# Emission by quarter-array products, and r, k, v loaded without padding

## The chip, the cores and the metric

The kernel runs on one core of a Trainium2 chip. The metric is the device time of one execution in microseconds (us). The core has five engines that work side by side: PE (TensorE, matrix products; the loading of weights is listed apart as PEld), DVE (VectorE), ACT (ScalarE), POOL (GpSimd) and SP (SyncE), which here only issues transfers. Each engine runs its own list of instructions strictly in order; between engines, semaphores hold an instruction back until what it reads is there.

## The reference

```python
for t in range(S):                       # B=4, H=8 heads, S=768, D=48
    cur = einsum('bhd,bhe->bhde', u[None] * k[t], v[t])
    y[t] = einsum('bhd,bhde->bhe', r[t], state + cur)
    state = w[None, :, :, None] * state + einsum('bhd,bhe->bhde', k[t], v[t])
x = y as 3072 rows of 384
e_idx = argmax(x @ w_gate)               # 8 experts; gate_w = softmax of the logits at e_idx
x = gate_w * sigmoid(x @ w_output_gate)[e] * (relu(x @ w1[e]) @ w2[e])
out = (silu(x @ m_gate) * (x @ m_val)) @ m_out      # 384 -> 1536 -> 384
```

So there is an attention with a decaying state and a bonus `u`, a mixture of eight experts with one expert for each token, and a gated feed-forward. Everything is float32.

## The kernel before

The first 132 us of the profiled execution are the attention, and what this text is about lies there. The 3072 tokens are 24 tiles of 128, six tiles to each of the four batches, in order. The eight heads stand as four pairs: in every transposed array a pair has one head on partitions 0 to 47 and the other on 64 to 111, and the rows between hold zeros. The host writes that padding into the input `tr` (r and k transposed, 128 partitions by 1024), and pads v to 64 columns a head in `tok`.

For tile i the work is this (names and lines are those of the profile; `yd_all` is one large array from which many buffers are carved, among them all loaded inputs, so they appear under its name):

- SP loads `tr` (L300), r and k by token (L301) and v (L305). There are three buffers for r and k and four for v, so the load of tile i+3 waits until all that reads tile i is done. The list of SP is written by hand and runs in order.
- `ck` = k·u·r (L396, L397), on DVE for tiles 0 to 2 and on POOL after that; its sum by head is `cb` (DVE, L419). POOL also makes `kdT` (L399) and `kdc` (L400), the scaled k; `kdc` needs `wk_tok`, a table made once at the start (L354, copied by ACT out of `pst`). DVE makes `rdT` (L407).
- ACT spreads `cb` over a diagonal, `dsb` (L423, eight instructions a tile), and DVE puts the scores `pss` (PE, L433) over its upper part (copy_predicated, L437).
- PE makes the new state `pskv` (L455; DVE adds it up in `st`, L465), and `psy` = state part (L482) + scores part (L489). ACT copies it as `yT` (L494).
- `emit` gives tile i out: four products of 32 columns, side by side in the array, for the 16 gate logits of each pair (`psl`, L114), four transposes of 128x128 (`psx`, L120), an ACT copy of each (`lT` L116, `xt` L122), the store of `xt` by SP (L123), a transpose back of the logits (`psl2`, listed as psl, L126) and a sum over the four pairs on DVE (`lg`, L127).

These run staggered: in round i come the scores of tile i, the state and output of tile i-1, and the emission of tile i-2. Between them DVE also works off the routing of the batches that are finished (L127 to L260) and the splitting of expert weights (L976). After the last tile's logits, the last routing step releases the experts and then the feed-forward.

At the start, before the first tile, the table of decay powers is made: `wc`, a scan by DVE (L339) and its reciprocals (L343), from these ACT's `wr_ps` (L345) and `we` (L349), then four transposes `pst` and the copy `wk_tok` (L354). [...]

Of the kernel before, what the change touches and what calls it, by code (L numbers as in the profile page):

```python
# [9 lines left out]
F32 = mybir.dt.float32  # L10
# [26 lines left out]
def moe_kernel(ctx, tc, cst, small, tok, tr, u, w1, w2, m_gate, m_val, m_out, out):  # L37
# [71 lines left out]

    def emit(yT, x_rows, lg, pool, ps_m, ps_y):  # L110

        psl = ps_m.tile([P, P], F32, name="psl", tag="m")
        for q in range(NP):
            nc.tensor.matmul(psl[32 * q : 32 * q + 32, :], lhsT=wg[:, q, :], rhs=yT[:, q, :], start=True, stop=True)  # L114
        lT = pool.tile([P, P], F32, name="lT")
        nc.scalar.copy(lT, psl)  # L116

        psx = ps_y.tile([P, H, 64], F32, name="psx", tag="y")
        for q in range(NP):
            nc.tensor.transpose(psx[:, 2 * q : 2 * q + 2, :].rearrange("p h d -> p (h d)"), yT[:, q, :], ident)  # L120
        xt = pool.tile([P, H, D], F32, name="xt")
        nc.scalar.copy(xt, psx[:, :, 0:D])  # L122
        nc.sync.dma_start(out=x_rows, in_=xt.rearrange("p h d -> p (h d)"))  # L123
# [142 lines left out]
    with ExitStack() as actx:  # L266
        actx.enter_context(tc.manual_schedule(engines={mybir.EngineType.SP}))
        acst = actx.enter_context(tc.tile_pool(name="acst", bufs=1))
        apool = actx.enter_context(tc.tile_pool(name="apool", bufs=2))
        ps_m = actx.enter_context(tc.tile_pool(name="ps_m", bufs=2, space=PSUM))  # L270
        ps_c = actx.enter_context(tc.tile_pool(name="ps_c", bufs=1, space=PSUM))
        ps_s = actx.enter_context(tc.tile_pool(name="ps_s", bufs=2, space=PSUM))
        ps_y = actx.enter_context(tc.tile_pool(name="ps_y", bufs=2, space=PSUM))
        ps_r = actx.enter_context(tc.tile_pool(name="ps_r", bufs=1, space=PSUM))
# [37 lines left out]

        u_tok = acst.tile([P, H, D], F32, name="u_tok")
        for i in range(NIO):
# [41 lines left out]

        st_b = [acst.tile([P, NP, 64], F32, name=f"st{i}") for i in range(2)]
        kdc_b = [acst.tile([P, H, 64], F32, name=f"kdc{i}") for i in range(3)]
# [55 lines left out]
        def bonus(i):  # L414
            if i >= NTILE:
                return
            r_t, k_t, rT, kT, rdT, kdT, ck, kdc = S[i]
            cb = apool.tile([P, H], F32, name="cb")
            nc.vector.reduce_sum(cb, ck, axis=AX.X)  # L419

            dsb = apool.tile([P, H, P], F32, name="dsb", bufs=3)
            for h in [*range(0, H, 2), *range(1, H, 2)]:
                nc.scalar.mul(dsb[:, h, :], ident, cb[:, h : h + 1])  # L423
            S[i] = rdT, kdT, kdc, dsb, heads(io_v[i % NV], 64)

        def scores(i):
            rdT, kdT, kdc, dsb, v_t = S[i]

            banks = [(ps_y, "y"), (ps_m, "m")] if i == 1 else [(ps_s, "s")] * 2
            pss = [pool.tile([P, NP, P], F32, name=f"pss{j}", tag=tag) for j, (pool, tag) in enumerate(banks)]  # L430
            for q, j in itertools.product(range(NP), range(2)):
                p0 = 64 * j
                nc.tensor.matmul(  # L433
                    pss[j][:, q, :], lhsT=kdT[p0 : p0 + 64, q, :], rhs=rdT[p0 : p0 + 64, q, :], start=True, stop=True
                )
# [36 lines left out]

        def outputs(i):

            rdT, kdT, kdc, dsb, v_t = S[i]
            c = i % NCH
            psy = ps_y.tile([P, NP, P], F32, name="psy", tag="y")
            if c > 0:
                for q in range(NP):
                    for j in range(2):  # L480
                        pr = slice(64 * j, 64 * j + 64)
                        nc.tensor.matmul(  # L482
                            psy[pr, q, :], lhsT=st_b[i % 2][pr, q, :], rhs=rdT[pr, q, :], start=(q == 0), stop=False,
                            skip_group_check=True,
                        )
            for q in range(NP):
                for j in range(2):
                    p0 = 64 * j
                    nc.tensor.matmul(  # L489
                        psy[p0 : p0 + 64, q, :], lhsT=v_t[:, 2 * q + j, :], rhs=dsb[:, 2 * q + j, :],  # L490
                        start=(c == 0 and q == 0), stop=(q == NP - 1), skip_group_check=True,
                    )
# [29 lines left out]
        def rows_out(i):  # L522
# [6 lines left out]
            lg, mx = lgs[g.start]  # L529
            yield from emit(S.pop(i), x_d[i * P : (i + 1) * P, :], lg[:, i - g.start, :], apool, ps_m, ps_y)  # L530
            if i + 1 == g.stop:
# [22 lines left out]
        with tc.manual_schedule(engines=set(engines)):  # L554
# [55 lines left out]
            for _ in range(KF - 4):  # L610
                next(head)
            moe.transposed(0, more, ps_y, "y")
            for _ in head:
# [83 lines left out]
    def sequential(c):  # L697
# [11 lines left out]
        with tc.For_i(0, B) as b:  # L709
            nc.vector.memset(st, 0.0)  # L710
            with tc.For_i(0, NCH) as ch:
                i = b * NCH + ch
                rk = sq.tile([P, 2, NP, P], F32, name="sq_rk")
                nc.sync.dma_start(
                    out=rk.rearrange("p a q t -> p (a q t)"), in_=tr[bass.ds(i, 1)].rearrange("o p n -> (o p) n")
                )
                yT = sq.tile([P, NP, P], F32, name="sq_y")
                nc.vector.memset(yT, 0.0)
                with tc.For_i(0, P) as t:
                    kv = sq.tile([P, NP, D], F32, name="sq_kv")  # L720
# [620 lines left out]
def _layout(inputs):  # L1341
# [6 lines left out]

    def tokens(a, pad=0):
        a = a.transpose(0, 2, 1, 3)  # L1350
        if pad:
            a = np.concatenate([a, np.zeros(a.shape[:3] + (pad,), a.dtype)], axis=3)
        return a.reshape(b * n, P, -1)

# [8 lines left out]
    def transposed(a):  # L1363
        a = a.reshape(b, h, n, P, d).transpose(0, 2, 1, 4, 3)
        return pair_rows(a, 0).reshape(b * n, P, -1)

# [6 lines left out]
        "small": small,  # L1373
        "tok": np.concatenate([tokens(r), tokens(k), tokens(v, 64 - d)], axis=2),
        "tr": np.concatenate([transposed(r), transposed(k)], axis=2),
        "u": u,
# [28 lines left out]
```

## Time and profile before

| what | us |
|---|---|
| time of the kernel, median of 3 runs | 837.77 (837.74 to 838.23) |
| time of the profiled execution | 840.54 |
| span of the profiled execution | 838.8 |
| PE / DVE / ACT / POOL busy in the span | 812.4 / 509.9 / 352.0 / 210.1 |
| mean granted clock of PE | 0.993 of full speed |

The profile is of one execution, which took 840.54 us, of which 838.8 us are the span from the first to the last instruction on record. Busy time counts neither waits nor the issue of transfers. PE is busy for 97% of the whole span, but that is a mean over stages in which other engines set the pace.

### The profile page before, as it was taken

To read this page: it belongs to the slowest core of one execution; us is meant where nothing else is said; L and a number is where in the kernel's file an instruction comes from. 1 tells how busy PE (TensorE), PEld (TensorE's weight loads), DVE (VectorE), ACT (ScalarE), POOL (GpSimd) and SP (SyncE) were. 2 spreads that over 40 slices of the span, in tenths; PEclk is the share of its full clock that TensorE was granted. 3 is DMA by queue.
4 is the path that set the end of the run, shared out by engine and by line. 5 is a ranking of instruction groups with operands and counts; after the bars stand their busy time and mean duration, and the time that the engine had idled before them with its cause. 6 is when DMAs were issued, how large, how long until landed. Compare 5 with 4: busy or idle time off the path is not lost.

```text
span 838.8 us, 14568 instructions
## 1 busy us (share of the span) xinstructions
PE 812.4 (97%) x5535; PEld 728.6 (87%) x5536; DVE 509.9 (61%) x1097; ACT 352.0 (42%) x794; POOL 210.1 (25%) x206
## 2 busy tenths in 40 slices
PE   7999999998999999999999999999999999999994
PEld 5777779898999999998888888888888888899994
DVE  7679996599998989855554235333433542344531
ACT  4878764565656566544332112212221221122321
POOL 7998951452433422200002000200100020000000
PEclk9999999999999999999999999999999999999998
DMA  8999974566878876432311000100000010000000
GB/s 309 313 335 327 346 240 136 156 195 198 262 238 253 252 239 205 122 102 86 90 52 47 5 1 13 38 1 1 32 20 1 7 38 1 0 19 27 20 1 23
DMA packets 61839, 99.57 MB, mean 119 GB/s; under 512 B 5364, under 2 KB 47872, under 8 KB 61760
## 3 DMA queue, kind: packets, MB, share of 16 engines
q1 hardware_dynamic: 58320, 88.44, 32.5%
q0 software_dynamic: 3440, 10.11, 3.7%
q8 instruction: 45, 0.74, 0.4%
q14 instruction: 34, 0.28, 0.1%
HBM read 82.00 MB, written 16.53 MB: 117 GB/s over the span
## 4 chain that ended last, share of the span: by engine, by line
issue 58%; DVE 15%; PE 11%; DMA 6%; POOL 5%; ACT 2%; SPq 0%; ACTq 0%; POOLq 0%; DVEq 0%
DMA m<-ab 2%; POOL out_dram L1245 2%; DVE w1l L976 2%; PE pss L433 2%; PE psy L489 2%; DVE ab L952 2%; PE psy L482 1%; DVE w2l L976 1%; DVE ab L948 1%; DMA r<-in_w_dram 1%; PE psx L120 1%; DVE ab L943 1%; DVE h L1121 1%; POOL xg L1053 1%; DMA yd_all<-in_tok_dram 1%
## 5 line engine op out<-in xcount | busy, mean ns | idle before, releaser
L1269 DVE TENSOR_TENSOR hv<-pg,hv 128x512 f32<-128x512 f32 (+1 forms) x84 | 51.7, 615 | 155.8 <-ACT hv L1268 155.7
L1245 POOL DMA_INDIRECT out_dram<-ot,tokd x24 | 24.8, 1035 | 452.2 <-DVE ot L1244 448.6
L1268 ACT ACTIVATE hv<-pg 128x512 f32<-128x512 f32 (+1 forms) x84 | 45.1, 537 | 168.3 <-PE pg L1264 168.0
L884 ACT CAST hh<-hv 128x512 fp32r<-128x512 f32 (+1 forms) x84 | 47.0, 559 | 142.1 <-DVE hv L1270 142.1
L1238 PE MATMUL po<-wh,hh 128*128 128x384 f32 x288 | 97.1, 337 | 0.0
L1238 PE MATMUL po<-wh,hl 128*128 128x384 f32 x288 | 97.0, 337 | 0.0
L1238 PE MATMUL po<-wl,hh 128*128 128x384 f32 x288 | 97.0, 337 | 0.0
L1264 PE MATMUL pg<-xh,wh 128*128 128x512 f32 (+1 forms) x252 | 91.1, 362 | 0.0
L1101 PE MATMUL ph<-x,w1h 128*128 128x416 f32 x336 | 91.1, 350 | 0.0
L1264 PE MATMUL pg<-xh,wl 128*128 128x512 f32 (+1 forms) x252 | 90.9, 361 | 0.0
L1264 PE MATMUL pv<-xh,wh 128*128 128x512 f32 (+1 forms) x252 | 90.8, 360 | 0.0
L1264 PE MATMUL pv<-xh,wl 128*128 128x512 f32 (+1 forms) x252 | 90.7, 360 | 0.0
L1264 PE MATMUL pv<-xl,wh 128*128 128x512 f32 (+1 forms) x252 | 90.6, 360 | 0.0
L1264 PE MATMUL pg<-xl,wh 128*128 128x512 f32 (+1 forms) x252 | 90.5, 359 | 0.0
L1101 PE MATMUL py<-h,w2h 128*128 128x416 f32 x336 | 89.7, 352 | 0.0
L885 DVE TENSOR_TENSOR hl<-hv,hh 128x512 fp32r<-128x512 f32 (+1 forms) x84 | 51.7, 616 | 45.4 <-ACT hh L884 45.1
L1270 DVE TENSOR_TENSOR hv<-pv,hv 128x512 f32<-128x512 f32 (+1 forms) x84 | 51.7, 615 | 43.7 <-PE pv L1264 43.1
L949 POOL TENSOR_TENSOR low<-low,exw 128x384 f32<-128x384 f32 x36 | 40.3, 1119 | 106.6 <-DVE exw L945 80.9
L423 ACT ACTIVATE dsb<-cs,cb 128x128 f32<-128x128 f32 x192 | 58.7, 390 | 14.2 <-DVE cb L419 14.2
L1101 PE MATMUL ph<-x,w1l 128*128 128x416 f32 x168 | 60.7, 361 | 3.3 <-DVE h L1121 3.3
L1101 PEld LDWEIGHTS py<-h,w2h 128*128 128x128 f32 x336 | 62.9, 188 | 0.8
L1101 PEld LDWEIGHTS ph<-x,w1h 128*128 128x128 f32 x336 | 63.0, 188 | 0.5
(228 smaller groups left out, 1710.2 us busy)
## 6 DMA issues: line engine op xcount, KB each, us to landing
r<-in_w_dram SPq DMA_DIRECT2D x64, 384.0 KB
yd_all<-in_tr_dram SPq DMA_DIRECT2D x24, 512.0 KB
yd_all<-in_tok_dram SPq DMA_DIRECT2D x24, 384.0 KB
m<-ab SPq DMA_DIRECT2D x36, 192.0 KB
rw<-m SPq DMA_DIRECT2D x36, 192.0 KB
yd_all<-in_tok_dram SPq DMA_DIRECT2D x24, 256.0 KB
x_d<-xt SPq DMA_DIRECT2D x24, 192.0 KB
cva<-in_w_gate_dram SPq DMA_DIRECT2D x12, 384.0 KB
```

The lines of the kernel that those rows point to most:

```text
L423: nc.scalar.mul(dsb[:, h, :], ident, cb[:, h : h + 1])
L884: first = nc.scalar.copy(hi, src)
L885: second = nc.vector.tensor_tensor(out=lo, in0=src, in1=hi.bitcast(F32), op=ALU.subtract)
L949: nc.gpsimd.tensor_tensor(out=low, in0=low, in1=ex.bitcast(F32), op=ALU.mult)
L976: nc.vector.tensor_tensor(out=lo, in0=r, in1=hi.bitcast(F32), op=ALU.subtract)
L1101: nc.tensor.matmul(dst[:, 0:n], lhsT=a, rhs=b, start=start and t == 0, stop=stop and t == 2)
L1238: nc.tensor.matmul(po[t], lhsT=a[:, t * P : (t + 1) * P], rhs=bb, start=(f == 0 and j == 0), stop=(f == KF2 - 1 and j == 2))
L1245: st = nc.gpsimd.indirect_dma_start(out=out[:, :], out_offset=bass.IndirectOffsetOnAxis(ap=tokd[:, i : i + 1].bitcast(U32), axis=0), in_=o ...
L1264: nc.tensor.matmul(dst, lhsT=a[:, fs], rhs=bb[:, q, :], start=(q == 0 and j == 0), stop=(q == KD - 1 and j == 2))
L1268: nc.scalar.activation(hv, pg, AF.Sigmoid)
L1269: nc.vector.tensor_tensor(out=hv, in0=pg, in1=hv, op=ALU.mult)
L1270: nc.vector.tensor_tensor(out=hv, in0=pv, in1=hv, op=ALU.mult)
```

## The change

The emission goes over to sixteen products of a quarter of the array each. For a pair q, head j (partitions 64j to 64j+47 of `yT`) and half k of the tokens (64k to 64k+63), one product of 48 rows by 64 tokens with a table `unit` of 64 columns gives 48 columns that are the head's transposed output and 16 that are its share of the logits. `unit` is an identity beside the gate weights, copied together by POOL at the start. So the psl products, the psx transposes and the psl2 transpose go away; ACT makes two copies from `psx` (`xt`, and `lh` with all logits, 128 values a token), and DVE sums eight parts instead of four.

The inputs lose their padding: `tr` comes as two transfers of 48 partitions (384 KB instead of 512 KB), v with 48 columns a head (192 KB instead of 256 KB). Partitions 32 to 63 and 96 to 127 of the three io buffers are set to zero once, by six DVE instructions ahead of everything else, and the loads into them follow. `st` and `pskv` have 48 columns, the products on 64 rows take 48. `psy` is one fixed bank, cleared once by DVE; `psx` has two banks of its own (pool ps_x), ps_m and ps_y shrink to one.

```diff
-    def emit(yT, x_rows, lg, pool, ps_m, ps_y):
-
-        psl = ps_m.tile([P, P], F32, name="psl", tag="m")
-        for q in range(NP):
-            nc.tensor.matmul(psl[32 * q : 32 * q + 32, :], lhsT=wg[:, q, :], rhs=yT[:, q, :], start=True, stop=True)
-        lT = pool.tile([P, P], F32, name="lT")
-        nc.scalar.copy(lT, psl)
-
-        psx = ps_y.tile([P, H, 64], F32, name="psx", tag="y")
-        for q in range(NP):
-            nc.tensor.transpose(psx[:, 2 * q : 2 * q + 2, :].rearrange("p h d -> p (h d)"), yT[:, q, :], ident)
-        xt = pool.tile([P, H, D], F32, name="xt")
-        nc.scalar.copy(xt, psx[:, :, 0:D])
...
-        psl2 = ps_m.tile([P, NP, 32], F32, name="psl2", tag="m")
-        nc.tensor.transpose(psl2.rearrange("p q e -> p (q e)"), lT, ident)
-        nc.vector.reduce_sum(lg, psl2[:, :, 0:G].rearrange("p q e -> p e q"), axis=AX.X)
+    unit = const.tile([P, NP, 64], F32, name="unit")
...
+    def emit(yT, x_rows, lg, pool, ps_x):
+        psx = ps_x.tile([P, 2, 8, 64], F32, name="psx", tag="x")
+        for q, (j, k) in itertools.product(range(NP), ((0, 0), (1, 1), (0, 1), (1, 0))):
+            pr, ts = slice(64 * j, 64 * j + D), slice(64 * k, 64 * k + 64)
+            nc.tensor.matmul(psx[ts, j, q, :], lhsT=yT[pr, q, ts], rhs=unit[pr, q, :], start=True, stop=True)
+        xt = pool.tile([P, NP, 2, D], F32, name="xt")
+        nc.scalar.copy(xt.rearrange("p q j d -> p j q d"), psx[:, :, 0:NP, 0:D])
+        nc.sync.dma_start(out=x_rows, in_=xt.rearrange("p q j d -> p (q j d)"))
+        lh = pool.tile([P, 2, NP, G], F32, name="lh")
+        nc.scalar.copy(lh, psx[:, :, 0:NP, D:])
+        yield
+        nc.vector.reduce_sum(lg, lh.rearrange("p j q e -> p e (j q)"), axis=AX.X)
...
-                nc.sync.dma_start(out=t[:, RK:], in_=tr[i])
+                for j in range(2):
+                    nc.sync.dma_start(out=t[64 * j : 64 * j + D, RK:], in_=tr[i, j])
...
-        u_tok = acst.tile([P, H, D], F32, name="u_tok")
+        for t in io:
+            for p0 in (32, 96):
+                nc.vector.memset(t[p0 : p0 + 32, RK:], 0.0)
+        u_tok = carve(H * D).rearrange("p (h d) -> p h d", d=D)
...
+        psy = ps_y.tile([P, NP, P], F32, name="psy", tag="y")
+        nc.vector.memset(psy, 0.0)
...
-            pskv = ps_m.tile([P, NP, 64], F32, name="pskv", tag="m")
+            pskv = ps_m.tile([P, NP, D], F32, name="pskv", tag="m")
```

The order of an engine's list is made by a scheduler when the kernel is built (SP's apart), and the change moves it at the start of two engines. First DVE, from the start of the program to the second `cb`. Before:

```order
L323 MEMSET ones 128x128
L334 MEMSET yd_all 128x4
L361 MEMSET rows_f 128x32
L362 MEMSET cum 128x4
L332 TENSOR_SCALAR wc<-sm_t 128x4
L339 SCALAR_TENSOR_TENSOR yd_all<-wc,ones 128x128 x4
L365 TENSOR_TENSOR wok<-wc,sm_t 128x4
L343 RECIPROCAL yd_all<-yd_all 128x128 x4
L320 CAST mask_b<-cs 128x128
L396 TENSOR_TENSOR ck<-yd_all,u_tok 128x384
L397 TENSOR_TENSOR ck<-ck,yd_all 128x384
L407 TENSOR_TENSOR rdT<-yd_all,wr_ps 128x512
```

After (without the small memsets and the first rows of the program; L409 is the first step of `ck`, L350 the scan, L354 the reciprocals, L432 is `cb`):

```order
L385 MEMSET psy 128x512
L343 TENSOR_SCALAR wc<-sm_t 128x4
L331 CAST mask_b<-cs 128x128
L409 TENSOR_TENSOR ck<-yd_all 128x384
L350 SCALAR_TENSOR_TENSOR yd_all<-wc,ones 128x128 x4
L376 TENSOR_TENSOR wok<-wc,sm_t 128x4
L409 TENSOR_TENSOR ck<-yd_all 128x384
L410 TENSOR_TENSOR ck<-ck,yd_all 128x384
L354 RECIPROCAL yd_all<-yd_all 128x128 x4
L410 TENSOR_TENSOR ck<-ck,yd_all 128x384
L420 TENSOR_TENSOR rdT<-yd_all,wr_ps 128x512
L432 TENSOR_REDUCE cb<-ck 128x8 x2
```

The first step of `ck` of tile 0, which reads the loaded `u`, now stands ahead of the scan and the reciprocals. Then ACT, its first instructions. Before:

```order
L345 ACT_TABLE_LOAD
L345 COPY wr_ps<-yd_all 128x512
L349 ACTIVATE we<-yd_all 128x128 x4
L354 COPY yd_all<-pst 128x384
L423 ACTIVATE dsb<-cs,cb 128x128 x24
L494 COPY yT<-psy 128x512
```

After (L365 is the copy of `wk_tok`, L436 is `dsb`):

```order
L356 ACT_TABLE_LOAD
L356 COPY wr_ps<-yd_all 128x512
L360 ACTIVATE we<-yd_all 128x128 x4
L436 ACTIVATE dsb<-cs,cb 128x128 x16
L365 COPY yd_all<-pst 128x384
L436 ACTIVATE dsb<-cs,cb 128x128 x8
L507 COPY yT<-psy 128x512
```

The copy of `wk_tok` now stands behind the `dsb` of tiles 0 and 1. POOL's list has `kdT` of tile 1 and 2 and then `kdc` of tiles 0, 1 and 2, which read `wk_tok`, ahead of the first `ck` of its own (tile 3).

## Rows read from the trace of the kernel before

**Rows 1.** Busy time by stretch: PE, PEld, DVE, ACT, POOL, PEclk, DMA share, GB/s.

```profile
30.00:60.00 30.00, 30.00 (x474) 24.01 (x474) 20.91 (x61) 23.25 (x73) 27.93 (x28) 1.00 0.93 320
47.45:118.77 71.32, 68.91 (x1075) 54.76 (x1073) 65.53 (x205) 55.75 (x167) 62.57 (x56) 1.00 0.96 332
118.77:132.30 13.53, 13.33 (x204) 10.56 (x203) 8.74 (x36) 7.24 (x22) 2.12 (x2) 1.00 0.25 80
```

**Rows 2.** Timeline of PE over one round: start, duration, engine, line, operation.

```profile
28.66 0.43 PE L114 MATMUL psl<-yT,sm_t 128*32 128x128 f32 x8
29.02 0.66 PE L120 MATMUL psx<-cs,yT 128*128 128x128 f32 x4
29.61 1.16 PE L433 MATMUL pss<-rdT,kdT 64*128 64x128 f32 x16
30.70 0.33 PE L126 MATMUL psl<-cs,lT 128*128 128x128 f32 x1
30.96 0.69 PE L455 MATMUL pskv<-yd_all,kdc 128*64 128x64 f32 x16
31.57 1.09 PE L482 MATMUL psy<-rdT,st 64*64 64x128 f32 x16
32.59 1.09 PE L489 MATMUL psy<-dsb,yd_all 128*64 128x128 f32 x16
33.62 0.43 PE L114 MATMUL psl<-yT,sm_t 128*32 128x128 f32 x8
```

**Rows 3.** Timeline of POOL: kdT of two rounds that follow each other.

```profile
28.23 1.28 POOL L399 TENSOR_TENSOR kdT<-yd_all 128x512 f32<-128x512 f32 x1
...
32.47 1.27 POOL L399 TENSOR_TENSOR kdT<-yd_all 128x512 f32<-128x512 f32 x1
```

**Rows 4.** Waits of DVE from 47.45 to 118.77: us in total, times, longest.

```profile
DVE dsb L437 <- PE pss L433: 2.2, 4, 0.9
...
DVE rk L176 <- PE bank L170: 1.1, 1, 1.1
```

**Rows 5.** Timeline of the start, DVE, ACT, POOL and SP; idle time before in brackets.

```profile
0.87 0.17 DVE L323 MEMSET ones<- 128x128 f32 x1 [0.75 <-PEq L1392]
...
0.99 0.06 DVE L334 MEMSET yd_all<- 128x4 f32 x1
...
2.96 1.37 DVE L339 TENSOR_TENSOR_SCAN yd_all<-wc,ones 128x128 f32<-128x128 f32 x4
...
4.30 3.38 DVE L343 RECIPROCAL yd_all<-yd_all 128x128 f32<-128x128 f32 x4
...
8.85 0.48 ACT L354 COPY yd_all<-pst 128x384 f32<-128x384 f32 x1 [0.73 <-PE pst L352]
...
9.44 0.63 DVE L396 TENSOR_TENSOR ck<-yd_all,u_tok 128x384 f32<-128x384 f32 x1 [1.68 <-DMA u_tok<-in_u_dram]
...
11.91 4.84 ACT L423 ACTIVATE dsb<-cs,cb 128x128 f32<-128x128 f32 x16 [2.59 <-DVE cb L419]
11.93 2.62 POOL L400 TENSOR_TENSOR kdc<-yd_all 128x384 f32<-128x384 f32 x2
...
13.30 0.33 SPq L301 DMA_DIRECT2D yd_all<-in_tok_dram  x1
...
17.70 1.00 POOL L396 TENSOR_TENSOR ck<-yd_all,u_tok 128x384 f32<-128x384 f32 x1 [0.65 <-DMA yd_all<-in_tok_dram]
```

**Rows 6.** Timeline of DVE: the two cb (tiles 9 and 23).

```profile
47.45 0.54 DVE L419 TENSOR_REDUCE cb<-ck 128x8 f32<-128x384 f32 x1
...
118.77 0.55 DVE L419 TENSOR_REDUCE cb<-ck 128x8 f32<-128x384 f32 x1
```

**Rows 7.** Groups of ACT from 20 to 132: busy, mean ns, idle before.

```profile
L122 ACT COPY xt<-psx 128x384 f32<-128x384 f32 x23 | 11.0, 479 | 3.1 <-ACT lT L116 2.2 <-PE psx L120 0.6 <-issue 0.2
L116 ACT COPY lT<-psl 128x128 f32<-128x128 f32 x24 | 6.4, 267 | 0.3 <-PE psl L114 0.3
```

More of the change, by code (lines that the diff above doesn't have):

```diff
@@ L108, in moe_kernel @@
     wg = sm_t[:, 2 * NP :].rearrange("p (q g) -> p q g", q=NP)
-    def emit(yT, x_rows, lg, pool, ps_m, ps_y):
-        psl = ps_m.tile([P, P], F32, name="psl", tag="m")
-        for q in range(NP):
-            nc.tensor.matmul(psl[32 * q : 32 * q + 32, :], lhsT=wg[:, q, :], rhs=yT[:, q, :], start=True, stop=True)
-        lT = pool.tile([P, P], F32, name="lT")
-        nc.scalar.copy(lT, psl)
-        psx = ps_y.tile([P, H, 64], F32, name="psx", tag="y")
-        for q in range(NP):
-            nc.tensor.transpose(psx[:, 2 * q : 2 * q + 2, :].rearrange("p h d -> p (h d)"), yT[:, q, :], ident)
-        xt = pool.tile([P, H, D], F32, name="xt")
-        nc.scalar.copy(xt, psx[:, :, 0:D])
-        nc.sync.dma_start(out=x_rows, in_=xt.rearrange("p h d -> p (h d)"))
+    unit = const.tile([P, NP, 64], F32, name="unit")
+    for j in range(2):
+        pr = slice(64 * j, 64 * j + 64)
+        nc.gpsimd.tensor_copy(
+            unit[pr, :, 0:D], ident[pr, 64 * j : 64 * j + D].rearrange("p (o d) -> p o d", o=1).to_broadcast([64, NP, D])
+        )
+    nc.gpsimd.tensor_copy(unit[:, :, D:], wg[:, :, 0:G])
+    def emit(yT, x_rows, lg, pool, ps_x):
[8 more added lines that the diff above has]
+        nc.scalar.copy(lh, psx[:, :, 0:NP, D:])
         yield
-        psl2 = ps_m.tile([P, NP, 32], F32, name="psl2", tag="m")
-        nc.tensor.transpose(psl2.rearrange("p q e -> p (q e)"), lT, ident)
-        nc.vector.reduce_sum(lg, psl2[:, :, 0:G].rearrange("p q e -> p e q"), axis=AX.X)
+        nc.vector.reduce_sum(lg, lh.rearrange("p j q e -> p e (j q)"), axis=AX.X)
     def route(sl, lg, mx, pool, ps, sm):
@@ L299, in load @@
                 t = io[i % NIO]
-                nc.sync.dma_start(out=t[:, RK:], in_=tr[i])
+                for j in range(2):
+                    nc.sync.dma_start(out=t[64 * j : 64 * j + D, RK:], in_=tr[i, j])
                 nc.sync.dma_start(out=t[:, 0:RK], in_=tok[i, :, 0:RK])
@@ L355, in moe_kernel @@
         nc.gpsimd.memset(yd_all[:, used[0] :], 0.0)
-        st_b = [acst.tile([P, NP, 64], F32, name=f"st{i}") for i in range(2)]
+        st_b = [acst.tile([P, NP, D], F32, name=f"st{i}") for i in range(2)]
         kdc_b = [acst.tile([P, H, 64], F32, name=f"kdc{i}") for i in range(3)]
@@ L423, in bonus @@
                 nc.scalar.mul(dsb[:, h, :], ident, cb[:, h : h + 1])
-            S[i] = rdT, kdT, kdc, dsb, heads(io_v[i % NV], 64)
+            S[i] = rdT, kdT, kdc, dsb, heads(io_v[i % NV])
         def scores(i):
             rdT, kdT, kdc, dsb, v_t = S[i]
-            banks = [(ps_y, "y"), (ps_m, "m")] if i == 1 else [(ps_s, "s")] * 2
-            pss = [pool.tile([P, NP, P], F32, name=f"pss{j}", tag=tag) for j, (pool, tag) in enumerate(banks)]
+            if i == 1:
+                both = ps_x.tile([P, 2, NP, P], F32, name="pss01", tag="x")
+                pss = [both[:, j] for j in range(2)]
+            else:
+                pss = [ps_s.tile([P, NP, P], F32, name=f"pss{j}", tag="s") for j in range(2)]
             for q, j in itertools.product(range(NP), range(2)):
[L432 to L435, printed above, removed]
+                pr = slice(64 * j, 64 * j + D)
+                nc.tensor.matmul(pss[j][:, q, :], lhsT=kdT[pr, q, :], rhs=rdT[pr, q, :], start=True, stop=True)
             for j in range(2):
@@ L476, in outputs @@
             c = i % NCH
-            psy = ps_y.tile([P, NP, P], F32, name="psy", tag="y")
             if c > 0:
@@ L489, in outputs @@
                     nc.tensor.matmul(
-                        psy[p0 : p0 + 64, q, :], lhsT=v_t[:, 2 * q + j, :], rhs=dsb[:, 2 * q + j, :],
+                        psy[p0 : p0 + D, q, :], lhsT=v_t[:, 2 * q + j, :], rhs=dsb[:, 2 * q + j, :],
                         start=(c == 0 and q == 0), stop=(q == NP - 1), skip_group_check=True,
@@ L529, in rows_out @@
             lg, mx = lgs[g.start]
-            yield from emit(S.pop(i), x_d[i * P : (i + 1) * P, :], lg[:, i - g.start, :], apool, ps_m, ps_y)
+            yield from emit(S.pop(i), x_d[i * P : (i + 1) * P, :], lg[:, i - g.start, :], apool, ps_x)
             if i + 1 == g.stop:
@@ L611, in moe_kernel @@
                 next(head)
-            moe.transposed(0, more, ps_y, "y")
+            moe.transposed(0, more, ps_x, "x")
             for _ in head:
@@ L713, in sequential @@
                 rk = sq.tile([P, 2, NP, P], F32, name="sq_rk")
-                nc.sync.dma_start(
-                    out=rk.rearrange("p a q t -> p (a q t)"), in_=tr[bass.ds(i, 1)].rearrange("o p n -> (o p) n")
-                )
+                nc.vector.memset(rk, 0.0)
+                for j in range(2):
+                    nc.sync.dma_start(
+                        out=rk[64 * j : 64 * j + D].rearrange("p a q t -> p (a q t)"),
+                        in_=tr[bass.ds(i, 1), j].rearrange("o p n -> (o p) n"),
+                    )
                 yT = sq.tile([P, NP, P], F32, name="sq_y")
@@ L1347, in _layout, with tokens @@
     n = s // P
[L1349 to L1353, printed above, removed]
+    def tokens(a):
+        return a.transpose(0, 2, 1, 3).reshape(b * n, P, -1)
     def pair_rows(a, fill):
@@ L1373, in _layout @@
         "small": small,
[L1374 to L1375 removed]
+        "tok": np.concatenate([tokens(r), tokens(k), tokens(v)], axis=2),
+        "tr": np.concatenate([transposed(r), transposed(k)], axis=3),
         "u": u,
```

21 lines of the change are left out of this document (11 added, 10 removed).

## The prediction

> **What bounds the kernel now.** I read the busy time by stretch first, since the mean over the span hides the stages. From 30 to 60 us PE is busy for all of its 30.00 us, DVE for 20.91 [rows 1]: here PE sets the pace. From 47.45 us (`cb` of tile 9) to 118.77 (`cb` of tile 23) [rows 6] two engines are nearly full: PE 68.91 and DVE 65.53 of 71.32 us, because DVE now has the routing of finished batches and the splitting of weights besides its tile work. POOL has 62.57 [rows 1]. From 118.77 to 132.30, the end of the attention, PE is busy for 13.33 of 13.53 us. So a gain on PE counts in full only where DVE and POOL follow, and each has a pace of its own. POOL's is in the timeline: from one `kdT` to the next 32.47 − 28.23 = 4.24 us, with its four instructions end to end [rows 3]. PE's round in the same place is 33.62 − 28.66 = 4.96 us [rows 2]. DVE's, from tile 9 on, is 65.53/14 = 4.68 us.
>
> The waits of DVE in that stretch say how much of its 71.32 − 65.53 = 5.8 us of idle time is PE's doing: 2.2 us for scores and 1.1 us for a routing product [rows 4]. The other 2.5 are waits that PE has no part in.
>
> After 132 us the program is the same work in both kernels, and it begins when the last logits are there. I take the shift at the end of the attention as the shift of the whole time.
>
> **PE's share of the change.** In the round of [rows 2], from start to start, `psl` takes 0.36, the transposes `psx` 0.59 and `psl2` 0.26: 1.21 us of emission go. What comes are 16 products, each as two instructions as all of PE's float32 work here (x16 stands for 8 products in the rows of `pss`): 32 instructions of 64 columns. The nearest row is `pskv`, 16 instructions of 64 columns on two halves of the array, which take 31.57 − 30.96 = 0.61 us, 76 ns for two side by side. The new ones use a quarter of the array each, in an order in which neighbours share neither rows nor columns. `psl`, four products on four quarters of the columns, took 0.36 us for eight instructions of 128 columns [rows 2]; two side by side would need four turns of twice 76 ns, 0.61 us, so four at a time do go. I take 32/4 × 76 ns = 0.61 us; the bounds are 0.61 and, two at a time, 1.22. Gain 0.60 us a round, lower bound 0. `pskv` of 48 columns for 64: 8 × 13 ns, worked from 0.61/8 = 76 ns by 16/64 and less what doesn't shrink, about 0.11 us (bounds 0 and 0.15). `pss` and `psy` stream the same 128 columns over fewer rows: 0. PE's round becomes 4.96 − 0.71 = 4.25 us, equal to POOL's 4.24.
>
> [...] The row: `pskv`'s 16 instructions run in 0.61 us, no more than one product's stream after the other [rows 2]. [...]
>
> **DVE's and ACT's share by tile.** `lg` sums 128 values for 64, four `st` instructions have 16 columns less each. From the two memsets of [rows 5], 0.17 us for 128 columns and 0.06 for 4, a column costs 0.11/124 = 0.9 ns: +0.06 and −0.06, nothing in sum (bounds −0.8 and +1.2 over 14 rounds, one edit alone with its set-up). ACT has `lh` for `lT`, the same 128 columns: 0.27 us [rows 7]; it is busy for 23.25 of 30 us and so has cover of 6.7. The loads: 1152 KB for 1344 a tile. The queues carry 320 GB/s in the loop [rows 1], but no wait in [rows 4] is for a load, so 0 for the steady rounds, and at the start only `u` counts, below.
>
> **The start.** This is the largest term, and it comes out of the moved instructions.
> - Six memsets of 1024 columns: 6 × 1024 × 0.9 ns = 5.5 us of DVE from 0.87 us on [rows 5]; with the small ones and the 512 columns of `psy` (0.5) DVE is free at about 7.4. Its next real work, `ck` of tile 0, started at 9.44, on `u` [rows 5]. I keep that (bounds 8.9, since less is loaded ahead of it, and 10.3, since the first `tr` loads now wait for memsets). So the memsets cost nothing while `u` is that late, and up to 5.5 us without this cover.
> - Behind that wait now stand scan and reciprocals, which ran from 2.96 to 7.68 us before [rows 5], in time that was free. Now: `ck` step 9.44 + 0.63 = 10.1; scan 1.37, 11.5; two more `ck` steps of 0.63, 12.8; reciprocals 3.38, 16.1; a `ck` step and `rdT`, 0.63 each, 17.4; first `cb`, by the 0.54 of [rows 6], 17.9.
> - ACT stands with its next instruction, `dsb`, on that `cb` (it started at 11.91 before), and its copy of `wk_tok` is queued behind 16 of them: 17.9 + 4.84 = 22.7, copy until 23.2 where it ended at 8.85 + 0.48 = 9.33 [rows 5].
> - POOL's `kdc` of tile 0 waits for `wk_tok`: 23.2 for 11.93, that is 11.3 later; three of about 1.0, as POOL's `ck` of 1.00, end at about 26.3.
> - The load of r and k of tile 3 needs the buffer that this `kdc` reads. It was issued at 13.30 and POOL's `ck` of tile 3 started on it at 17.70 [rows 5], 4.4 later, with other traffic around it. Now the issue is at 23.2 + 1.0 = 24.2. I estimate 3.1 us, nearer to 4.4 than to nothing since less else is under way (bounds 2.1, the time until POOL is free anyway, and 4.4): `ck` of tile 3 at 27.3 for 17.70, **+9.6** (bounds +8.0 and +11.8 with those of `u`).
>
> **The loop.** From there POOL is the slowest list up to tile 9. `ck` of tile 9 starts six rounds later, 27.3 + 6 × 4.24 = 52.7, and ends 2.0 later at 54.8 (its two steps of 1.00); `cb` of tile 9 at 54.9 for 47.45 [rows 6], +7.4: PE's faster round has given 2.2 us back. From tile 9 DVE is the floor: 65.5 us of work and 2.5 of waits that PE has no part in, 68.0 for 71.32: `cb` of tile 23 at 54.9 + 68.0 = 122.9 for 118.77, **+4.1**.
>
> **The tail.** Two emissions shorten by 0.60 each, one `pskv` by 0.11: −1.3. The last tile's logits pass more: `psx` 0.61 for `psl` 0.36, then ACT's `xt` of 0.48 ahead of `lh`, without `psl2`'s 0.33 [rows 2, 7]: +0.4. Together **−0.9** (bounds −1.9, if ACT takes nothing of it, and 0).
>
> Sum: 4.1 − 0.9 = +3.2 us. Against the profiled execution of 840.54 that gives 843.7; the median of the runs lies 2.77 below their profiled one, so 837.77 + 3.2 = **841.0**.
>
> **The rivals.** 0.2% (1.7 us, 836.1 to 839.4) is about what a measurement of this kernel tells from no change.
> - *Main: late start, partly recovered.* +1.7 to +5.5 by the bounds above. Chance 0.56.
> - *The quarters go two at a time.* Then PE's round falls by 0.11 only and PE bounds throughout: 9.6 − 21 × 0.11 − 2.4 (the gaps of PE, 71.32 − 68.91) = +4.9, 842.7. For it: the weight loads are 24.01 of 30 us already [rows 1], so a doubled load count can tell. Against it: the eight `psl` instructions in 0.36 us. Chance 0.12. [...]
> - *DVE loses all of its idle time.* If the 2.5 us of other waits were late effects of PE's pace too, `cb` of tile 23 comes at 54.9 + 65.5 = 120.4, +1.6, less 0.9: +0.7, 838.5, no change that can be told. For it: a large part of the idle time has several causes at once, and a wait is put down to the last. Chance 0.19.
> - *DVE is no floor (faster).* If DVE's instructions themselves shorten when PE and ACT press less on the same memories, the loop falls to PE's pace: 9.6 − 21 × 0.71 + 0.4 = −4.9, 832.9. It decides when DVE's 65.5 us come to 61.6 or less: 54.9 + 61.6 + 2.5 = 119.0, and with the tail less than 0. For it: nothing in the rows shows how much of an instruction's duration is contention. Against it: it takes 6% of all DVE work. Chance 0.13.
>
> **How the numbers follow.** The main case and the two-at-a-time case are slower: 0.56 + 0.12 = 0.68. The third is same: 0.19. The last is faster: 0.13. The range leaves out the faster case and the outer ends of the main one: 837.9 to 844.5. The main one's own range is 839.5 to 843.3.
>
> **What would show it.** `ck` of tile 0 at 9 to 10 us with scan and reciprocals behind it; `wk_tok` copied near 23 us; POOL's `ck` of tile 3 near 27; the sixteen `psx` products in about 0.6 us; `kdT` to `kdT` 4.24 without gaps up to 50 us; `cb` of tile 9 near 55 and of tile 23 near 123, with DVE over 90% busy between; the attention's end near 135.5. I am wrong if POOL's `ck` of tile 3 starts under 23 us, if the emission takes over 1 us, or if DVE's busy time between the two `cb` falls below 62 us.

## The result

The changed kernel takes 845.33 us (median of 4 runs, 844.52 to 847.69) against 837.75 us before (4 runs, 837.16 to 838.23): 1.0099 times the time, 95% interval 1.0081 to 1.0117. That is 7.6 us slower where 3.2 were forecast, and outside the range of 837.9 to 844.5. Timed once more in the last set (e17, below) the ratio was 1.0133 [1.0118, 1.0149].

### The profile page after: what moved, and what is told of

It is laid out like the page before. It is cut to its first block, busy times and chain, and to the rows that moved or that the text cites. A ratio compares the mean times of both kernels' runs of the same rounds, so it can differ in the third digit from the quotient of the medians.

```text
span 843.5 us, 15541 instructions
## 1 busy us (share of the span) xinstructions
PE 807.0 (96%) x5991; PEld 728.8 (86%) x5992; DVE 514.9 (61%) x1104; ACT 350.8 (42%) x794; POOL 210.2 (25%) x209
## 4 chain that ended last, share of the span: by engine, by line
issue 58%; DVE 11%; POOL 4%; DMA 4%; PE 4%; ACT 1%; SPq 0%; POOLq 0%; DVEq 0%; ACTq 0%
DMA m<-ab 4%; POOL out_dram L1261 2%; DVE w1l L992 2%; DVE ab L968 2%; DVE ab L964 1%; DVE w2l L992 1%; DVE ab L959 1%; PE pya L1117 1%; DVE h L1137 1%; DVE low L967 1%; POOL xg L1069 1%; DVE exw L961 1%; POOL low L965 1%; PE pha L1117 1%; DVE x L901 1%
## 5 line engine op out<-in xcount | busy, mean ns | idle before, releaser
L436 ACT ACTIVATE dsb<-cs,cb 128x128 f32<-128x128 f32 x192 | 58.6, 388 | 26.0 <-DVE cb L432 25.9
```

## The profile after

The start went as forecast, step by step. Timeline of the changed kernel, start and duration in us, idle time before in brackets (L409 is the first step of `ck`, L350 the scan, L354 the reciprocals, L436 `dsb`, L365 the copy of `wk_tok`, L413 `kdc`); compare [rows 5]:

```profile
9.50 0.56 DVE L409 TENSOR_TENSOR ck<-yd_all 128x384 f32<-128x384 f32 x1 [0.59 <-DMA yd_all<-in_u_dram]
9.98 1.78 DVE L350 TENSOR_TENSOR_SCAN yd_all<-wc,ones 128x128 f32<-128x128 f32 x4
...
13.27 3.38 DVE L354 RECIPROCAL yd_all<-yd_all 128x128 f32<-128x128 f32 x4
...
18.15 4.78 ACT L436 ACTIVATE dsb<-cs,cb 128x128 f32<-128x128 f32 x16 [1.06 <-DVE cb L432]
...
22.84 0.46 ACT L365 COPY yd_all<-pst 128x384 f32<-128x384 f32 x1
...
23.37 3.06 POOL L413 TENSOR_TENSOR kdc<-yd_all 128x384 f32<-128x384 f32 x3 [3.54 <-ACT yd_all L365]
...
26.88 0.37 SPq L308 DMA_DIRECT2D yd_all<-in_tok_dram  x1
...
27.73 1.00 POOL L409 TENSOR_TENSOR ck<-yd_all 128x384 f32<-128x384 f32 x1 [1.30 <-DVE st L474]
...
32.55 0.69 PE L125 MATMUL psx<-unit,yT 48*64 48x64 f32 x32
33.18 1.16 PE L449 MATMUL pss<-rdT,kdT 48*128 48x128 f32 x16
...
34.25 1.00 POOL L409 TENSOR_TENSOR ck<-yd_all 128x384 f32<-128x384 f32 x1 [2.24 <-DMA yd_all<-in_tok_dram]
```

`ck` of tile 0 waits for `u`, scan and reciprocals stand behind it, `wk_tok` comes at 23.3, and POOL's `ck` of tile 3 at 27.73, where 27.3 was forecast. The 32 instructions of the emission run in 33.18 − 32.55 = 0.63 us; 0.61 was forecast. The first surprise is the last line: `ck` of tile 4 waits 2.24 us for its `tok`, issued at 26.88 and used at 34.25.

Then the loop. The `cb` of tiles 9 and 23 in the timeline of DVE, against [rows 6], and the busy times between and behind them (PE, PEld, DVE, ACT, POOL, PEclk, DMA share, GB/s), against [rows 1]:

```profile
57.54 0.55 DVE L432 TENSOR_REDUCE cb<-ck 128x8 f32<-128x384 f32 x1 [1.31 <-POOL ck L410]
...
128.46 0.54 DVE L432 TENSOR_REDUCE cb<-ck 128x8 f32<-128x384 f32 x1
```

```profile
57.54:128.46 70.92, 63.16 (x1303) 52.93 (x1301) 66.11 (x204) 53.86 (x164) 63.96 (x58) 0.98 1.03 301
128.46:141.98 13.52, 11.74 (x279) 9.85 (x277) 9.40 (x37) 6.94 (x21) 2.12 (x2) 1.00 0.24 71
```

The reader is to see three things. The stretch takes 70.92 us, hardly less than the 71.32 of before, though PE's work fell from 68.91 to 63.16. DVE is busy for 66.11 of it. And the DMA engines are full (share 1.03) at 301 GB/s, where 332 went through at 0.96 before. The tail has kept its 13.5 us with 11.7 us of PE in it.

What DVE and POOL waited for in that stretch; first POOL before the change, then DVE and POOL in the changed kernel (us in total, times, longest):

```profile
POOL ck L396 <- DMA yd_all<-in_tok_dram: 3.3, 2, 2.0
```

```profile
DVE cb L432 <- POOL ck L410: 3.5, 4, 1.4
...
POOL ck L409 <- DMA yd_all<-in_tok_dram: 1.8, 1, 1.8
```

DVE now waits for POOL's `ck`, of which the view of before shows nothing in that stretch (1.31 of the 3.5 us lie just ahead of it, in the line of 57.54 above). POOL itself waited for `tok` in both kernels, and longer before.

What SP waited for between 27 and 118 us in the changed kernel (us in total, times, longest); before, no wait of SP in that time was for a transfer:

```profile
SPq L307 <- DMA yd_all<-in_tok_dram: 6.4, 10, 1.0
SPq L308 <- DMA r<-in_w_dram: 5.8, 4, 1.9
...
SPq L307 <- DMA r<-in_w_dram: 3.4, 4, 2.0
...
SPq L128 <- DMA yd_all<-in_tr_dram: 3.0, 9, 0.5
```

In all rows of that view its waits for transfers come to 31.8 us; all 57 of them end with the landing of the transfer issued eight before.

## The experiments

Eighteen runs were made, in five sets; each set ran on one chip beside the kernel before, and ratios are to that. The second and the fifth set had the same chip. "By hand" means that the start is put in the order of before: scan, reciprocals and the copy of `wk_tok` first, `unit` copied by ACT.

### First set: start, loads, emission

e1, before with the memsets alone:

```diff
+        for t in io:
+            for p0 in (32, 96):
+                nc.vector.memset(t[p0 : p0 + 32, RK:], 0.0)
```

> The kernel before with nothing but the six memsets of 32x1024 ahead of its loads (padded loads, old emission). The order that is built then is nearly that of the changed kernel: first step of ck ahead of scan and reciprocals, the copy of wk_tok behind eight dsb instead of sixteen. Theory START (the late start is the loss, and the loop cannot make it up because PE, DVE, POOL and the loads are all nearly full in it): POOL's ck of tile 3 near 25 to 27 us for 17.70, the time 843 to 847. Theory TRANSFERS (the smaller transfers bring fewer bytes a second, and the loads set the loop's pace; the start would be made up): 837.5 to 840.

1.0076 [1.0063, 1.0089]. The scheduler moves the start nearly as in the changed kernel, POOL's `ck` of tile 3 comes at 23.81 (25 to 27 was expected), and the loop takes it along: `cb` of tile 9 at 53.35 for 47.45, of tile 23 at 125.62 for 118.77. The late start alone is worth 6.4 us.

e2, the changed kernel with the start by hand:

```diff
-                nc.vector.memset(t[p0 : p0 + 32, RK:], 0.0)
+                (nc.vector if p0 == 32 and n < 2 else nc.gpsimd).memset(t[p0 : p0 + 32, RK:], 0.0)
...
-        actx.enter_context(tc.manual_schedule(engines={mybir.EngineType.SP}))
+        actx.enter_context(tc.manual_schedule(engines={
+            mybir.EngineType.SP, mybir.EngineType.PE, mybir.EngineType.DVE, mybir.EngineType.Activation, mybir.EngineType.Pool}))
```

> The changed kernel with the start in an order written by hand: scan, reciprocals and the copy of wk_tok first, as before the change; two of the six memsets on DVE and four on POOL; unit copied by ACT behind wk_tok. Loop untouched. START: ck of tile 3 at 17 to 20 us, the time 834 to 838. TRANSFERS: the loop still takes about 71 us from cb of tile 9 to that of tile 23, DMA share over 1.0 at 300 GB/s, the time 841 or more.

1.0061 [1.0038, 1.0085], with runs from 837.8 to 848.3. START expected 834 to 838: the early order is back (first `cb` at 11.59), but the loss is not gone. Nor is the start as early as before: POOL's `ck` of tile 3 comes at 20.99, where 17 to 20 was expected. POOL waits 8.3 us for `tok` in this trace. So there is more than the order of the start.

e3, the changed kernel with `tr` in one transfer:

```diff
-                for j in range(2):
-                    nc.sync.dma_start(out=t[64 * j : 64 * j + D, RK:], in_=tr[i, j])
+                nc.sync.dma_start(out=t[:, RK:], in_=tr[i])
```

> The changed kernel with tr loaded as before, one transfer of 128 partitions and 512 KB instead of two of 48 partitions and 384 KB together; memsets and late start stay. START: as the changed kernel, 843.5 to 847. TRANSFERS: the loop gets 2 us or more shorter, the waits of POOL on tok shrink, 839 to 843.

1.0157 [1.0119, 1.0196], no better than the changed kernel; the runs go from 845.6 to 859.1 around a median of 848.3, a little over what START expected. In the time, the loads' form did not show with the late start in place. In the trace it did, if only by 1.3 us: from `cb` of tile 9 to that of tile 23 it is 69.64 us for the 70.92 of the changed kernel, where TRANSFERS expected 2 or more.

```profile
56.88:126.52 69.64, 62.65 (x1301) 52.86 (x1299) 66.89 (x204) 53.74 (x164) 64.60 (x58) 0.98 0.95 326
```

e4, before with the new `emit` and its PSUM pools alone (as in the diff of the change), start by hand:

> The kernel before with the new emission alone (padded loads, no memsets, products on 64 rows), its start written by hand as in e2. Both theories: no late start and old transfers, so what is left is the emission: by PE's 0.60 us a round with DVE at 4.68 a round as the floor I expect 833 to 837.5. If it is not faster than 837.8, the gain on PE is hidden altogether.

0.9996 [0.9987, 1.0005]. The faster emission is worth nothing that can be told. Its stretch from `cb` of tile 9 to that of tile 23 says why:

```profile
46.27:116.44 70.17, 62.94 (x1337) 54.03 (x1335) 67.31 (x205) 54.38 (x166) 63.51 (x58) 1.00 0.98 348
```

PE needs 62.94 us, but DVE needs 67.31, more than the 65.53 of before: the sum `lg` over 128 values takes a median of 358 ns, that over 64 took 213.

### Second set: rows and transfers apart, all on e4

e5 (with the fixed `psy`, and `st` and `pskv` of 48 columns) and e6, which also packs v (`V = H * D`):

```diff
-                        pr = slice(64 * j, 64 * j + 64)
+                        pr = slice(64 * j, 64 * j + D)
```

e7 has the two transfers of 48 partitions and the memsets of e2; e8:

```diff
-                nc.sync.dma_start(out=t[:, RK:], in_=tr[i])
+                for j in range(2):
+                    nc.sync.dma_start(out=t[64 * j : 64 * j + 64, RK:], in_=tr[i, 64 * j : 64 * j + 64])
```

> e4 (new emission, padded loads, start by hand, 837.25) with the products of 48 rows instead of 64, st and pskv of 48 columns and the one fixed psy; loads stay padded. Theory TRANSFERS (what e2 loses against e4 comes from the smaller loads): 836.5 to 838. Theory ROWS (PE does less in the same time with 48 rows, gets a lower granted clock at times, and the time scatters): 839 to 845, mean granted clock 0.985 or less in several runs, over 3 us between its runs.

> e5 with v packed as well (192 KB for 256 KB a tile, rows of 1536 B). From here to e2 only the two transfers of 48 partitions for tr and the six memsets are missing. TRANSFERS by the v loads: 838.5 or more; by the tr loads alone: as e5. ROWS: as e5.

> e4 with tr in two transfers of 48 partitions (384 KB for 512 KB) and the six memsets, of which two lie on DVE and four on POOL ahead of the start; products stay on 64 rows, v padded. TRANSFERS: under 310 GB/s at a DMA share of 1.0 from 40 to 120 us, POOL waits 5 us or more on tok, 839.5 to 844. ROWS: 836.5 to 838.

> e4 with tr in two transfers of 64 partitions each, padded as before: the same bytes, one transfer more a tile. If the number of transfers costs: as e7. If it is the 48 partitions: as e4, 836.5 to 838.

e5 1.0038 [1.0024, 1.0052]; e6 1.0033 [1.0014, 1.0053]; e7 1.0098 [1.0067, 1.0129]; e8 1.0282 [1.0261, 1.0303]. TRANSFERS is borne out by e7 (its 848.6 us are even above the 839.5 to 844 expected, on a chip where the kernel before takes 840.3) and by e8, which neither guess foresaw and which is the clearest: the same bytes, only in two halves of the partitions, cost 2.8%. e5 and e6 are slower by 0.3 to 0.4%, as ROWS has it; the fourth set shows why that does not settle it. Busy time from 40 to 110 us in e7, then in e8, then in e4:

```profile
40.00:110.00 70.00, 61.73 (x1254) 52.23 (x1248) 58.14 (x172) 50.94 (x155) 58.35 (x55) 0.95 1.00 279
```

```profile
40.00:110.00 70.00, 59.60 (x1177) 50.15 (x1173) 53.48 (x153) 46.33 (x141) 52.46 (x50) 0.93 1.01 279
```

```profile
40.00:110.00 70.00, 64.34 (x1379) 55.29 (x1378) 66.16 (x195) 57.00 (x174) 67.38 (x61) 1.00 0.97 343
```

With half-height transfers the DMA engines are full at 279 GB/s (share 1.00 in e7, 1.01 in e8), with full height they bring 343 at 0.97 (e4). In e8 POOL waits 18.9 us for `tok`.

The slow loading also delays the start, with the order written by hand and, in e8, without a memset: POOL's `ck` of tile 3 comes at 22.07 in e7 and 22.74 in e8 for 17.27 in e4, `cb` of tile 9 at 55.28 and 55.23 for 46.27. So "by hand" is not free of a late start where the transfers are half height, and of the 20.9 us that e8 has lost at `cb` of tile 23 (137.34 for 116.44), 9.0 lie ahead of tile 9.

And the clock. In e5 PE was busy for 1.6 to 1.7 of each 2 us from 98 to 106 us, and then its granted clock fell from 1.00 to 0.50 for some 13 us:

```profile
98.00:100.00 2.00, 1.71 (x46) 1.22 (x42) 1.97 (x7) 1.40 (x5) 2.00 (x3) 1.00 0.82 214
100.00:102.00 2.00, 1.68 (x32) 1.56 (x34) 1.97 (x6) 2.00 (x8) 1.92 (x3) 1.00 0.92 357
102.00:104.00 2.00, 1.57 (x52) 1.25 (x46) 2.00 (x5) 1.26 (x4) 2.00 (x2) 1.00 0.62 225
104.00:106.00 2.00, 1.66 (x20) 1.38 (x22) 2.00 (x5) 2.00 (x8) 1.92 (x3) 1.00 0.96 270
106.00:108.00 2.00, 2.00 (x28) 1.88 (x30) 2.00 (x5) 1.64 (x6) 2.00 (x2) 0.51 0.96 373
...
116.00:118.00 2.00, 2.00 (x22) 1.61 (x20) 1.90 (x8) 0.00 (x0) 0.14 (x1) 0.50 0.96 350
118.00:120.00 2.00, 2.00 (x44) 1.55 (x42) 1.89 (x6) 0.63 (x2) 0.00 (x0) 0.58 0.11 40
```

The fall comes where DVE is busy for 1.97 to 2.00 of each 2 us, so that PE has gaps: from 98 to 106 us it waits 0.22, 0.39 and 0.70 us for DVE. Not every stretch with gaps is like this: in e4 PE is busy for 62.94 of 70.17 us at a clock of 1.00. And the 48 rows are not needed for it: e8 and e15, on 64, have mean clocks of 0.93 (above) and 0.95 in the loop.

### Third set: count or height, rows or columns

e9 is e4 with `tr` in two transfers of all 128 partitions (r and k apart); e10 is e7, and e11 e2, with v and x moved for two tiles at once; e12 is e6 with scores and state part on 64 rows.

```diff
+                for j in range(2):
+                    nc.sync.dma_start(out=t[:, RK + T * j : RK + T * j + T], in_=tr[i, :, T * j : T * j + T])
```

e10 and e11, for v, and in the same way for x; e12 is e5's diff taken back:

```diff
-                nc.sync.dma_start(out=io_v[i % NV], in_=tok[i, :, RK:])
+                nc.sync.dma_start(
+                    out=io_vp[i % NV // 2].rearrange("p (a n) -> p a n", a=2),
+                    in_=tok[i : i + 2, :, RK:].rearrange("a t n -> t a n"),
+                )
```

> e4 with tr in two transfers of all 128 partitions, r and k apart (256 KB each): the bytes of e4, one transfer more a tile, full height. SP issues a transfer only when the eighth one before it has landed. Theory COUNT (with a sixth transfer in the round SP stands on that rule, loads come late whatever their shape): as e8, 1.02 to 1.03 of the kernel before, SP's waits for transfers 25 us or more between 27 and 118 us. Theory HEIGHT (transfers over 64 or 48 partitions are slower in themselves): as e4, 0.998 to 1.002.

> e7 (tr in two transfers of 48 partitions, 1.0098) with v loaded for two tiles at once and x stored for two tiles at once: the same bytes, the four transfers a tile of the kernel before instead of five (stores counted). COUNT: SP's waits for transfers fall from 38 us to under 10, the time to 0.998 to 1.004 of the kernel before. HEIGHT: stays at 1.007 to 1.013.

> The whole change with the start by hand (e2, 1.0061), and v and stores two tiles at a time as in e10. COUNT: what is left is e6's rows of 48 alone, 1.001 to 1.004. HEIGHT: as e2, 1.004 to 1.009.

> e6 (v packed, padded tr, start by hand, 1.0033) with the scores and the state part on 64 rows again, 48 columns as in e6. Theory ROWS (48 of 64 rows in these two products bring the lower granted clock): 0.996 to 1.000, clock 0.987 or more, spread under 3 us. If it is the fixed psy or the 48 columns of pskv and psy: as e6, 1.002 to 1.005.

e9 0.9999 [0.9990, 1.0009]; e10 1.0096 [1.0062, 1.0130]; e11 1.0090 [1.0056, 1.0124]; e12 0.9994 [0.9983, 1.0005]. My theory COUNT had come from SP's 31.8 us of waits, and it falls on both sides: one more transfer a tile costs nothing at full height, and one fewer gains nothing at half height. HEIGHT stands. Busy time of e9 over the same 70 us, with 28 transfers of 256 KB for `tr` where e8 has 24:

```profile
40.00:110.00 70.00, 66.00 (x1379) 56.71 (x1379) 65.37 (x191) 56.92 (x175) 66.97 (x61) 0.98 0.96 336
```

SP's waits in the changed kernel are thus taken as the echo of slow transfers: with `tr` at half height the DMA engines moved 279 GB/s (e7, e8), at full height 336 (e9) and 343 (e4). Why half height is slower no run here shows.

e12 has everything of the change but the two transfers, the 48 rows and the memsets, and is equal to before.

### Fourth and fifth set: how the causes go together

e13 is e3 with scores and state part on 64 rows, e14 is e2 with these, e15 the changed kernel with these; e16 and e18 repeat e3, e17 the changed kernel.

> e3 (late start as in the changed kernel, tr in one transfer of 128 partitions, v packed) with scores and state part on 64 rows. Of the three causes only the start is left. If the three stand side by side: as e1, 1.005 to 1.0085, spread under 4 us. If e3's excess over the changed kernel came from its loads or start and not from the rows: 1.012 or more.

> e2 (whole change, start by hand) with scores and state part on 64 rows. Only the transfers of half height are left: 1.003 to 1.011; between 40 and 110 us under 300 GB/s at a DMA share of 1.0. If half height is hidden once PE runs at its full clock: 0.998 to 1.002.

> The changed kernel with scores and state part on 64 rows: start and half height are left. If the causes overlap (the late start and slow loads wait for the same thing): 1.006 to 1.009. If they add up: 1.012 to 1.018. If the rows are worth what e12 against e6 shows: 0.003 to 0.004 below the changed kernel's 1.0099.

> e3 once more, unchanged. If its 1.0157 was the scatter that goes with 48 rows: 1.008 to 1.014. If full height is really no better with the late start: 1.013 to 1.019.

> The changed kernel as it is, beside e18 on one chip. Runs on different chips have differed in how long the first expert stage waits for its gathered tokens, so that e3 and e16 (1.016 and 1.018) may not be comparable with the 1.0099 measured for the changed kernel alone. If so: 1.015 to 1.02 here, within 0.003 of e18. If full height is really the worse of the two with a late start: 1.008 to 1.012, 0.005 or more below e18.

> e3 and e16 once more (changed kernel, tr in one transfer of 128 partitions), beside e17. 1.014 to 1.019. The ratio of e17 to it tells what half height is worth behind a late start: above 1.002 it costs, below 0.998 it gains, between these it is hidden by the late start.

| | start | tr | rows | ratio |
|---|---|---|---|---|
| e13 | late | full height | 64 | 1.0136 [1.0114, 1.0157] |
| e14 | by hand | half | 64 | 1.0088 [1.0058, 1.0118] |
| e15 | late | half | 64 | 1.0158 [1.0139, 1.0178] |
| e16 | late | full height | 48 | 1.0177 [1.0150, 1.0204] |
| e17 | late | half | 48 | 1.0133 [1.0118, 1.0149] |
| e18 | late | full height | 48 | 1.0153 [1.0130, 1.0175] |

e13 to e16 ran on one chip, e17 and e18 on another. On the first, lateness alone is 1.0136 and half height alone 1.0088, and both together 1.0158, not their sum: behind a late start most of the slow loading is hidden. (1.0158 lies where e15 was expected if the causes add up, but that range took lateness from e1; here it measured 1.0136, outside the 1.005 to 1.0085 of e13.) e17, which came between its two guesses, and e18 say the same of the changed kernel: in the time, its half-height transfers and full-height ones cannot be told apart there. The traces show a rest: from `cb` of tile 9 to that of tile 23 it is 69.6 to 69.8 us with a late start and full height (e3, e13, e16, e18), and 70.8 to 72.1 with a late start and half height (the changed kernel, e15, e17). The pair on one chip, e17 and then e18:

```profile
59.15:129.94 70.79, 64.33 (x1301) 54.34 (x1299) 67.84 (x205) 53.63 (x164) 63.16 (x58) 0.95 1.02 296
```

```profile
59.15:128.98 69.83, 62.69 (x1301) 52.93 (x1299) 67.13 (x204) 53.73 (x164) 63.90 (x58) 0.98 0.94 326
```

The 48 rows: e16 lies 0.0041 above e13 on the same chip, with mean granted clocks of 0.973 to 0.985 for 0.988 to 0.990, but the two intervals touch. In the third set it is the other way round, 1.0090 for e11 on 48 rows and 1.0096 for e10 on 64. e15 against e17 is on two chips and says nothing on this.

The chips differ. The traces of e3 and e16 are of one kernel; behind the attention PE waits for the gathered tokens of the first expert stage, in e3 and then in e16 (us in total, times, longest):

```profile
PE pt L1079 <- DVE x L897: 1.2, 1, 1.2
```

```profile
PE pt L1079 <- DVE x L897: 3.5, 1, 3.5
```

The whole stage behind the attention differs. From the first expert product to the first product of the feed-forward, the one kernel of e3, e16 and e18 takes 241.6, 245.1 and 245.9 us on its three chips. In the traces of the first and third set it is 240.1 to 242.3, in the others 245.1 to 247.0, and in the one trace of the kernel before 243.3. So ratios within a set can be compared, and ratios of two sets not to a few tenths of a per cent. This is why e5 and e6 do not settle ROWS: in e6 the first expert product comes at 131.2 us, before the 132.3 of the kernel before, and the whole loss lies behind it, on the chip of the second set.

## Why the prediction was wrong

**The start: right.** Place, order and size of the delay came out to half a microsecond (27.73 for 27.3), and e1 shows that a late start decides the sign: memsets alone, with old loads and old emission, make the kernel slower by 0.76%.

**PE's emission: right.** 0.63 us for 0.61; the rival with two at a time, 1.22, is out. In `pskv`'s row all products use all rows of the array, and yet 0.55 us of weight loads (below, from the trace of before) lie within the 0.61 us that its sixteen instructions take from start to start, so that products ran beside them. In the emission 0.56 us of weight loads lie within the 0.63 us (32.55 to 33.18 in the trace of the changed kernel).

```profile
30.96 0.55 PEld L455 LDWEIGHTS pskv<-yd_all,kdc 128*64 128x64 f32 x16
```

**The step that failed: "no wait in [rows 4] is for a load, so 0 for the steady rounds".** [rows 4] shows waits of DVE alone. In the same stretch POOL waited 3.3 us for `tok` before the change (the line in the section on the profile after), and the DMA engines stood at a share of 0.96 [rows 1]: nearly full. So loads were a limit already, only one that DVE did not see. (The "1152 KB for 1344" also count the store of 192 KB; the loads are 960 for 1152.) The term that this put at nothing lies between `ck` of tile 3 and `cb` of tile 9, where the sum has six rounds of 4.24 us and nothing else. The loads of tiles 3 to 5, all held by the late `kdc`, were issued together between 24.5 and 29.5 us, `tok` of tile 4 was used 7.4 us after its issue, and POOL stood 2.24 us for it. The rounds after that took the 4.24. So `cb` of tile 9 came at 57.54, not 54.9: 0.4 from the start and 2.2 from this wait. Full height takes away only a part of it: from `ck` of tile 3 to `cb` of tile 9 it is 28.3 to 29.8 us in the four late starts with full height (e3, e13, e16, e18) and 29.2 to 30.4 in the three with half height (the changed kernel, e15, e17), for the 27.6 of the sum. That the bunching does the rest is argued; no run issues these loads apart.

**The floor was mis-sized: 70.92 us for "65.5 us of work and 2.5 of waits", 68.0.** Work was 66.11, 0.6 more, and idle time 4.8, 2.3 more, with DVE now waiting for POOL. But the same kernel has 67.84 and 2.95 in e17: how the miss divides between work and waits changes from one execution to the next, the miss itself hardly (70.79). With full-height loads behind the same late start the stretch takes 69.64 (e3, work 66.89, idle 2.75). So of the 2.9 us 1.3 go with half height (1.0 by e17 and e18), 1.6 are left without it, and 1.4 of these are DVE's work. What the sum had wrong there is `lg`: it costs 358 − 213 = 145 ns more and not 60, 2.0 us over 14 rounds, so that the emission's gain of 0.6 us a round on PE ends on DVE; in e4, where loads and start are as before, DVE has 67.31 us of work and the stretch takes 70.17. I took the cost of a column, 0.9 ns, from memsets; in the sum the 64 values more cost 145/64 = 2.3 ns each.

Half height had no term in the sum. It cost 1.0 to 2.5 us of the loop behind a late start, which the time hardly shows, and 0.9 to 1.0% of the time with the start by hand (e7, e10, e14), part of it as a late start of its own.

**The tail: −0.9 forecast, nothing came.** 141.8 − 128.5 = 13.3 us for 13.5. PE has less work there (11.74 of 13.52 us), but waits in turn, 0.8 us of it for `lh`. That the longer chain of the last logits, the +0.4 of the sum, ate the gain is a reading that no run tests.

**What is later given back.** The experts' first product comes 9.5 us later (141.8 for 132.3), the feed-forward's first 7.2 (382.8 for 375.6). "I take the shift at the end of the attention as the shift of the whole time" is off by 2.3 us: in the profile of before PE has gaps of 1.2 us from 200 to 210 and 0.8 from 290 to 300, waiting for other engines, and in those of the changed kernel there are none in these stretches. The 7.2 agree with the 7.6 of the medians. (The spans of the two profiled executions differ by 4.7 only, 838.8 and 843.5: from the last product of that kind to the end it is 15.6 us before and 13.1 after.) Whether the 2.3 belong to the change is open, since this stage alone differs by more from chip to chip.

So the sum is, in terms of the trace: 3.2 forecast, +0.4 start, +2.2 first loads, +2.9 floor, +0.7 tail, −2.3 given back, 7.1. The sum before the last term is 9.4; that the total misses by no more is due to the 2.3, which the prediction did not foresee.

**The rivals.** Two at a time: out. DVE loses all its idle time: out, it kept 4.8 of 5.8 us. DVE is no floor: out, e4 shows the floor by itself. None of them held the case that came, which was the main one with the loads as a further limit and a higher floor.

**What stays open.** Why the late start costs 1.36% with the new emission and packed v (e13) and 0.76% with the old ones (e1). The two were on different chips, and little of it lies in the attention: the first expert product comes at 140.5 us in e13 and 139.1 in e1, and the stage behind it takes 245.1 for 240.1. Whether the kernel before is as slow there on that chip no trace shows. What the 48 rows cost in the changed kernel, if anything: no two runs show it clear of noise or chip.

## What to carry to other kernels

When a change moves the start of a pipeline that three engines and the loads run almost full, price the delay at its full size and do not count on catching up (in e1 `ck` of tile 3 came 6.1 us later, and the time was 6.4 longer): look at the DMA share and at the waits of every engine, not only of the one that is the floor. Cutting the padding out of `tr` was no saving here, where each of its transfers then covered 48 partitions (e7: 384 KB for 512, 279 GB/s at a DMA share of 1.00 for the 343 at 0.97 of e4, and 1.0098 of the time); compare GB/s at a full DMA share, not bytes. And give a start that matters its order by hand, since six memsets at its head were enough to reorder three engines (POOL's list moved too: `kdT` of tile 2 now stands ahead of `kdc` of tile 0).

## What the hardware showed that I had not expected

- Two transfers of 64 partitions for one of 128, same bytes: 279 GB/s at a share of 1.01 for 343 at 0.97, and 2.8% of the whole time, 9.0 us of it ahead of tile 9 (e8, beside e4). The same split by columns: 336 GB/s and nothing (e9).
- In e5 PE had gaps of 0.3 to 0.4 us in each 2 us from 98 to 106 us, and then a granted clock of 0.50 for some 13 us. In e4 it had gaps too (busy for 62.94 of 70.17 us) and kept 1.00; what sets the clock no run shows. Some of the kernels also scatter more than the one before (e2: 837.8 to 848.3, the one before on the same chip 836.3 to 839.4); why, no run shows.
- One kernel on three chips took 241.6, 245.1 and 245.9 us for one and the same stage, from the first expert product to the first of the feed-forward (e3, e16, e18), at a mean granted clock of 0.99 in all three.
